# The first two units of the first batch with a 128-row third factor, filter copies without a double write, and second-factor reads ahead of the x loads

## The chip, the cores and the metric

The kernel runs on one core of a Trainium2 chip. The metric is the device time of one execution in microseconds (us), the median of several runs. The engines are named as in the profile: PE (TensorE, with PEld for its weight loads), DVE (VectorE), ACT (ScalarE), POOL (GpSimd) and SP (SyncE, which issues nearly all DMAs). SPq and POOLq are the DMA queues of SP and POOL. A DMA that waits for a semaphore holds up everything behind it on its queue.

## The reference

A spectral filter over the sequence, then a two-layer network with ELU:

```python
# x (8, 3008, 256); filt_r, filt_i (1505, 256)
X = np.fft.rfft(x, axis=1)
Y = X * (filt_r + 1j * filt_i)[None]
y = np.fft.irfft(Y, n=3008, axis=1).astype(np.float32)   # (8, 3008, 256)
# moe_w_in (256, 2048), moe_w_out (2048, 256); both arrive in 64-bit floats
h = y.reshape(24064, 256) @ moe_w_in
g = np.where(h > 0, h, np.exp(np.minimum(h, 0)) - 1)
out = (g @ moe_w_out).astype(np.float32)                 # (24064, 256)
```

## The kernel before

3008 = 47 x 64, and the two transforms are done as products with small tables. For each batch `b` there are four steps. The first factor (`x_load`, `x_unit`, `a_unit`) goes over the 64 positions and writes `z` to DRAM (`z_write`, line 309). The second factor reads `z` back by frequency (`z_read`, line 315), multiplies with its table (`b_unit`, line 384), with the filter (`re_mult` to `im_sums`, DVE), and with the back table (`bi_unit`, line 456); `y_write` (line 467) writes the rows to `yds[b]` in DRAM. The third factor reads them by `n1` (`y_read`, line 480) with a table `tn` (`tn_read`, line 473), and `n_unit` (line 495) makes the time-domain rows of six units `m` of a batch, each of 4 `n1` pairs. The network takes each unit in four parts `q` of the hidden width. Unit and part together are a *quad*, 24 for a batch.

The network's products use a seven-product scheme on 2x2 blocks. `n_sums` (lines 505 to 515) makes the block sums that the scheme needs from the unit's result; `up_steps` (line 538) does seven products with `w_in` in the order 1, 2, 6, 5, 7, 3, 4, then ELU on ACT and DVE; `down_steps` (line 620) does seven products with `w_out`. `c_unit` and `o_unit` combine and store (line 669). All matmuls are in 32-bit floats; each shows as two records in the profile.

`n_unit` as it is: the rows of frequency stand in two halves of 64 partitions, even and odd, and every product is one of four 64x64 tiles of PE, 32 matmuls in all. It yields `even` and `odd` parts in two banks, both complete only at the end; `n_sums` joins them with five DVE instructions, the first over two blocks at once. The first up product needs the result of that first instruction.

The first batch is started by its own functions (lines 245 to 371, 808 to 907): `a_first`, `t_first`, `b_first`, `bi_first`, with `y_write_first` at its end. Then come `y_read(0, 0, ...)` in two parts (line 884), the last weight blocks (`w_fetch(14)`, `w_fetch(15)`), some vector work on weights (`w_split`, `w_float`, `w_join`), warming matmuls (line 898), `x_load(1, 0)` and `(1, 1)`, `n_unit(0, 0)` and `n_sums(0, 0)`. The weights come as 64-bit floats and are turned into 32-bit floats on ACT and DVE; that work reaches into the first four quads.

Nothing is reordered by a scheduler. The order is written by hand: `at(quad, place, fn, ...)` puts a call into a plan, where place 0 is the middle of the quad, 1 its end and 2 and 3 spots between its products. The main loop goes over the quads and emits products and planned calls. All SP queue entries thus stand in program order. For batch `b`, whose quads start at `t + PER` with `t = (b - 1) * PER`, the plan makes the second factor during the quads of the batch before: `a_unit`, `z_write` and the next `x_load`s from quads `t + 0` (for batch 1: 2) to `t + 4`, `z_read` at `t + 5` place 0 for the first pair of groups, `b_unit` at `t + 6` place 1. At quad 4 the order on SP was `z_write` (4 DMAs), two `x_load`s (14 DMAs), and then, from quad 5, `z_read` (8 DMAs).

`f_pairs` (lines 768 to 776) runs at quads 1 to 4 and lays the filter out anew in DRAM, from `fd` to `fp`. For `u == 0` it wrote row 0 of the second half twice: zeros for all groups (`nil_d`), and then the true row for group 0. The second write waits for the first.

Of the kernel before, what the change touches and what calls it, by code (L numbers as in the profile page):

```python
# [26 lines left out]
P = 128  # L27
# [4 lines left out]
K2 = 32  # L32
# [9 lines left out]
def _make_tables():  # L42

    n2, k2 = np.arange(N2), np.arange(K2)
    ta, tn = np.zeros((P, H, P)), np.zeros((P, H, P))
    for i in range(H):
        for h in range(2):
            if h and i == 0:
                continue  # L60
            n1 = N1 - i if h else i
            th = 2 * np.pi * (((N1 * n2[:, None] + n1) * k2[None]) % N) / N
            c, s = np.cos(th), -np.sin(th)
            c[:, 0], s[:, 0] = 1.0, 1.0 - 2.0 * (n2 % 2)
            sign = -1.0 if h else 1.0
            r = slice(h * 64, h * 64 + 64)
            for p, v in enumerate((c, sign * s, s, sign * c)):
                ta[r, i, p * 32:p * 32 + 32] = v
                tn[p * 32:p * 32 + 32, i, r] = v.T
    tf = np.ascontiguousarray(ta.reshape(P, H, 4, K2).transpose(0, 1, 3, 2)).reshape(P, H, P)  # L70
    tb = ta.reshape(2, 2, 32, NXC, 2, 2, 4, 16, 2)[:, 0].transpose(3, 0, 1, 2, 4, 7, 5, 6)
    ta = np.ascontiguousarray(tb).reshape(P, H // 2, P)
    i = np.arange(H)[:, None]
    gb, gr, gi = (np.zeros((P, 2, 64)) for _ in range(3))
    q = np.arange(N1)[None]
    th = 2 * np.pi * ((i * np.where(q < 24, q, 70 - q)) % N1) / N1
    c, s = np.cos(th), np.sin(th)
    sign = np.where(q < 24, 1.0, -1.0)
    gb[0:24, 0, :N1], gb[24:48, 0, :N1] = c, s
    gb[64:88, 0, :N1], gb[88:112, 0, :N1] = c * sign, -s * sign  # L80
    for o in (0, 64):
        gr[o:o + N1, 0, 0:24], gr[o:o + N1, 0, 24:48] = 2 / N * c.T, 2 / N * s.T
        gi[o:o + N1, 0, 0:24], gi[o:o + N1, 0, 24:48] = 2 / N * (c * sign).T, -2 / N * (s * sign).T
    k1 = np.arange(24)[None]
    t0 = 2 * np.pi * ((i * k1) % N1) / N1
    t3 = 2 * np.pi * ((i * (32 + 64 * k1)) % N) / N
    c0, s0, c3, s3 = np.cos(t0), np.sin(t0), np.cos(t3), np.sin(t3)
    gb[0:24, 1, 0:24], gb[24:48, 1, 24:48] = c0, c3
    gb[64:88, 1, 24:48], gb[88:112, 1, 0:24] = -s3, -s0

    m0, m3 = np.full((24, 1), 2 / N), np.full((24, 1), 2 / N)
    m0[0] = m3[23] = 1 / N
    s0[:, 0] = s3[:, 23] = 0.0
    gr[0:24, 1, 0:24], gr[24:48, 1, 24:48] = m0 * c0.T, m3 * c3.T
    gi[0:24, 1, 24:48], gi[24:48, 1, 0:24] = -m0 * s0.T, -m3 * s3.T

    fb, bb = np.zeros((P, 2, 32)), np.zeros((P, 2, 4, 32))
    for p in range(4):  # L100
        r = slice(32 * p, 32 * p + 24)
        fb[r, 0, :24] = (-1.0 if p == 3 else 1.0) * gb[24 * (p % 2):24 * (p % 2) + 24, 0, 0:24]
        q = (0, 24, 64, 88)[p]
        k = 24 if p in (1, 2) else 0
        fb[r, 1, :24] = gb[q:q + 24, 1, k:k + 24]
    for o in range(0, P, 32):
        for p, (t, c) in enumerate(((gr, 0), (gr, 24), (gi, 0), (gi, 24))):
            bb[o:o + 24, 0, p, :24] = t[0:24, 0, c:c + 24]

    bb[0:24, 1, 0, :24], bb[0:24, 1, 1, :24] = gr[0:24, 1, 0:24], gr[24:48, 1, 24:48]  # L110
    bb[0:24, 1, 2, :24], bb[0:24, 1, 3, :24] = gi[24:48, 1, 0:24], gi[0:24, 1, 24:48]
    pairs = np.concatenate([fb.reshape(P, 64), bb.reshape(P, 2 * P)], 1)
    lie = np.concatenate([2 * np.arange(24), 2 * np.arange(24) + 1])
    gb[:, :, lie] = gb[:, :, :48].copy()
    for t in (gr, gi):
        for o in (0, 64):
            t[o + lie] = t[o:o + 48].copy()
    gf = np.zeros_like(gb)
    for o in (0, 64):
        gf[o:o + 48] = gb[o:o + 48].reshape(2, H, 2, 64).swapaxes(0, 1).reshape(48, 2, 64)  # L120
    tn = tn.reshape(4, K2 // 2, 2, H, 2, 2, 32)[..., 0, :] * np.array([1.0, -2.0])[:, None, None, None]
    tn = np.ascontiguousarray(tn.transpose(2, 1, 0, 3, 4, 5)).reshape(P, H, 64)
    once = np.stack([np.eye(P), gf.reshape(P, P)], 1)
    return [t.astype(np.float32) for t in (ta, tn, np.stack([gb, gr, gi], 1), tf, once, pairs)]


def order(m):
# [5 lines left out]
def kernel(  # L133
# [8 lines left out]
):  # L142
    nc = tc.nc

    ta_d, tn_d, gs_d, tf_d, once_d, pairs_d = [
        nc.inline_tensor(t, name=n + "_t").ap()
        for t, n in zip(_make_tables(), ("ta", "tn", "gs", "tf", "once", "pairs"))
    ]

    def pool(name, bufs, **kw):  # L150
# [311 lines left out]
    def y_write(b, g):  # L462
# [3 lines left out]
        for p in range(4):  # L466
            nc.sync.dma_start(yds[b][4 * g:4 * g + 8, 24 * p:24 * p + 24, :].rearrange("u r d -> r u d"),
                              t[32 * p:32 * p + 24])

    def tn_read(b, m):  # L470
        w = tnp.tile([P, 4, P], FP32, tag="tn", name="tn").rearrange("p a (q t) -> p (a q) t", t=64)[:, 0:4]
        tns[b, m] = w
        nc.sync.dma_start(w, tn_d[:, 4 * m:4 * m + 4, :])

    def y_read(b, m, *parts):
        t = t4s[b, m] = t4p.tile([P, 4, D], FP32, tag="t4", name="t4")
        for k in parts or (slice(0, K2),):
            for r in range(2):
                o = 64 * r
                nc.sync.dma_start(t[o + 2 * k.start:o + 2 * k.stop].rearrange("q i d -> q (i d)"),  # L480
                                  yds[b][k.start + r:k.stop:2].rearrange("k (p i) d -> k p (i d)", p=4)
                                  [:, :, 4 * m * D:4 * m * D + 4 * D])

    def half(m):

        return 224 if m == 0 else 256

    def n_unit(b, m):
        t, w, h = t4s.pop((b, m)), tns.pop((b, m)), half(m)
        ps = [bank("psn", (P, 2, 256)) for _ in range(2)]  # L490
        for q, i in enumerate(order(m)):
            for dh in range(2):
                for c in range(2):
                    for (_, p), r in zip(ps, HALVES):
                        nc.tensor.matmul(p[ts(c, 64), dh, ts(q, 64)], t[r, i - 4 * m, ds(dh * P + 64 * c, 64)],  # L495
                                         w[r, i - 4 * m, :], start=True, stop=True)
        even, odd, both = (yp.tile([P, 2, 256], FP32, tag=n, name=n)[:, :, 0:h] for n in ("y0", "y1", "yb"))
        t2 = yp.tile([P, 256], FP32, tag="yt", name="yt")[:, 0:h]
        ys[b, m] = {1: both[:, 0], 2: both[:, 1], 3: even[:, 1], 4: odd[:, 1], 5: odd[:, 0], 6: t2, 7: even[:, 0],
                    "even": even, "odd": odd, "both": both}  # L500
        for t, (k, p) in zip((even, odd), ps):
            nc.scalar.activation(out=t, in_=p[:, :, 0:h], func=AXT.Copy)
            banks.append(k)

    def n_sums(b, m, *parts):
        even, odd, both, t2 = (ys[b, m][k] for k in ("even", "odd", "both", 6))
        steps = ((both, odd, -0.5, even, ALU.add), (even[:, 1], odd[:, 1], 0.5, even[:, 1], ALU.add),
                 (t2, even[:, 1], 1.0, odd[:, 0], ALU.subtract), (even[:, 0], t2, 1.0, both[:, 0], ALU.subtract),
                 (odd[:, 1], both[:, 1], 1.0, t2, ALU.subtract))
        for i in parts or range(5):  # L510
            o, x, c, y, op = steps[i]
            if c == 1.0:
                nc.vector.tensor_tensor(out=o, in0=x, in1=y, op=op)
            else:
                nc.vector.scalar_tensor_tensor(out=o, in0=x, scalar=c, in1=y, op0=ALU.mult, op1=op)  # L515
# [252 lines left out]
    def f_pairs(c, u):  # L768

        src = fd.rearrange("g a q c u d -> (g a) q c u d")[:, :, c, u, :]  # L770
        dst = fp.rearrange("g (a u) k c h d -> (g a) u k c h d", u=2)[:, u, :, c, :, :]
        nc.sync.dma_start(dst[:, :, 0, :], src[:, 0:48:2, :])
        nc.sync.dma_start(dst[:, 1:24, 1, :], src[:, 1:46:2, :])
        nc.sync.dma_start(dst[:, 0, 1, :], nil_d)
        if u == 0:
            nc.sync.dma_start(dst[0, :, 1, :], src[0, 1:48:2, :])

    with tc.manual_schedule():
# [152 lines left out]
        for b in range(B):  # L931
            t = (b - 1) * PER
            if b > 0:
                for c, s in enumerate((2, 2, 3, 3, 4, 4) if b == 1 else (0, 0, 3, 3, 4, 4)):
# [4 lines left out]
                    if c % 2:  # L939
                        for k in (c - 1, c):  # L940
                            at(t + s, 1, z_write, b, k)
                        for k in (c - 1, c):
                            nb, nxt = (b, k + XBUFS) if k + XBUFS < NXC else (b + 1, k + XBUFS - NXC)
                            if nb < B:
                                at(t + s, 1, x_load, nb, nxt)
                for g in range(0, NG, 2):
                    s = t + 6 + 2 * g
                    opens.update((s + 1, s + 4))
                    for k in (g, g + 1):
                        at(s - 2, 1, f_read, b, k)  # L950
                        at(s - 1, 0, z_read, b, k)
                    at(s, 1, b_unit, b, g)
                    at(s + 1, 2, re_mult, b, g)
                    at(s + 1, 1, re_sums, b, g)
# [81 lines left out]
```

## Time and profile before

| | us |
|---|---|
| median of 3 runs | 2572.96 |
| lowest, highest | 2567.81, 2576.67 |
| profiled execution, whole | 2571.72 |
| its span (first to last instruction) | 2569.9 |
| PE busy in the span | 2525.8 |
| DVE busy | 2069.0 |
| ACT busy | 1545.1 |
| POOL busy | 159.5 |
| n_unit(0, 0): first matmul, most of them from | 86.59, 87.70 |
| first up product | 90.97 |
| first b_unit (batch 1) | 180.98 |

All times inside the profile are counted from the start of the span. The profile's page gives busy time of each engine, the chain of work that ended last (followed back from the last instruction), groups of instructions and DMA issues. The trace can be asked further: for instructions in order of time, for what an engine waited for, and for busy time in given stretches, with the clock that PE was granted (PEclk, 1.00 is full) and the share of time in which the core's 16 DMA engines were busy. The end of a matmul is modelled, so a PE that stands still shortly between matmuls can still show as busy; the start times tell it.

### The profile page before, as it was taken

The page shows a single profiled execution, that of the slowest core. Times are in us where ns is not written, and L with a number is a line of the kernel's source. Part 1 is how long each engine was busy: PE and PEld are TensorE (multiplying, and loading weights), DVE is VectorE, ACT ScalarE, POOL GpSimd, SP SyncE. Part 2 cuts the span into 40 slices and gives each one's busy share as a digit, 9 for nine tenths or more (in the row PEclk, how much of TensorE's full clock was granted, in tenths as well). Part 3 has the DMA queues.
Part 4 walks back from the last instruction along what each step waited for, and adds up shares of the span by engine and source line. Part 5 has one row for each costly group of instructions (what it writes and reads, how often), then busy time and mean ns, then how long its engine had stood idle before and what let it go on. Part 6 is the DMA issues. An engine that isn't in the chain of part 4 may idle for free.

```text
span 2569.9 us, 44172 instructions
## 1 busy us (share of the span) xinstructions
PE 2525.8 (98%) x16778; PEld 2167.7 (84%) x16778; DVE 2069.0 (81%) x3580; ACT 1545.1 (60%) x2715; POOL 159.5 (6%) x315
## 2 busy tenths in 40 slices
PE   6899999999999999999999999999999999999998
PEld 4688889888898888988889888888888888898887
DVE  6878887788877888788887888778897788876766
ACT  6665655666566655665566656566656655555554
POOL 5000100010000000000000000000000011000000
PEclk8999999999999999999999999999999999999999
DMA  9563213422234231433215231243213322110010
GB/s 279 166 177 79 69 26 91 130 68 57 49 89 118 59 74 44 111 85 75 60 40 148 67 81 36 75 122 82 57 44 83 85 63 68 36 46 19 19 28 17
DMA packets 229948, 200.36 MB, mean 78 GB/s; under 512 B 129418, under 2 KB 202314, under 8 KB 229736
## 3 DMA queue, kind: packets, MB, share of 16 engines
q1 hardware_dynamic: 214376, 166.65, 26.2%
q0 software_dynamic: 14000, 30.44, 4.2%
q8 instruction: 132, 2.16, 0.4%
q10 hardware_dynamic: 1360, 0.46, 0.1%
q14 instruction: 80, 0.66, 0.1%
HBM read 125.58 MB, written 78.17 MB: 79 GB/s over the span
## 4 chain that ended last, share of the span: by engine, by line
PE 96%; DMA 2%; DVE 1%; issue 0%; SPq 0%; ACT 0%; DVEq 0%; ACTq 0%
PE po L620 45%; PE phs L538 25%; PE phd L538 13%; PE pha L538 6%; PE psn L495 2%; PE pf L384 2%; PE psa L235 2%; PE pv L456 1%; DMA xc<-in_x_dram 1%; DMA x<-in_x_dram 0%; DMA yd<-t 0%; PE po L331 0%; PE po L297 0%; PE psr L331 0%; PE psa L278 0%
## 5 line engine op out<-in xcount | busy, mean ns | idle before, releaser
L620 PE MATMUL po<-g,wo 128*128 128x256 f32 (+1 forms) x5376 | 1319.1, 378 | 0.0
L620 PEld LDWEIGHTS po<-g,wo 128*128 128x128 f32 x5376 | 1013.2, 190 | 164.9 <-issue 50.5
L549 ACT ACTIVATE g<-phs 128x512 f32<-128x512 f32 (+1 forms) x576 | 338.7, 588 | 739.9 <-PE phs L538 737.9
L556 ACT ACTIVATE e<-e 128x512 f32<-128x512 f32 (+1 forms) x768 | 477.2, 621 | 24.3
L560 DVE SCALAR_TENSOR_TENSOR g<-e,g 128x512 f32<-128x512 f32 (+1 forms) x576 | 387.6, 673 | 13.6 <-ACT e L556 13.2
L546 DVE TENSOR_TENSOR g<-phd,g 128x512 f32<-128x512 f32 (+1 forms) x384 | 258.9, 674 | 168.0 <-ACT e L556 110.2
L538 PE MATMUL phd<-y,wi 128*128 128x256 f32 (+1 forms) x1536 | 388.6, 376 | 3.4 <-DVE g L546 3.4
L538 PE MATMUL phs<-y,wi 128*128 128x256 f32 (+1 forms) x1536 | 387.8, 375 | 0.6 <-ACT g L549 0.6
L555 ACT ACTIVATE e<-g 128x512 f32<-128x512 f32 (+1 forms) x576 | 354.5, 615 | 35.8 <-DVE g L546 27.1
L538 PEld LDWEIGHTS phd<-y,wi 128*128 128x128 f32 x1536 | 291.2, 190 | 39.3 <-DVE g L546 7.0
L538 PEld LDWEIGHTS phs<-y,wi 128*128 128x128 f32 x1536 | 292.1, 190 | 33.7 <-ACT g L549 1.2
L560 DVE SCALAR_TENSOR_TENSOR g<-e,phs 128x512 f32<-128x512 f32 (+1 forms) x192 | 130.0, 677 | 114.6 <-ACT e L556 114.6
L538 PE MATMUL phs<-yb,wi 128*128 128x256 f32 (+1 forms) x768 | 194.9, 377 | 1.8 <-DVE yb L515 1.8
L538 PE MATMUL phs<-yt,wi 128*128 128x256 f32 (+1 forms) x768 | 194.4, 376 | 0.9 <-ACT g L549 0.9
L538 PE MATMUL pha<-yb,wi 128*128 128x256 f32 (+1 forms) x768 | 194.6, 376 | 0.0
L555 ACT ACTIVATE e<-phs 128x512 f32<-128x512 f32 (+1 forms) x192 | 112.2, 584 | 111.5 <-PE phs L538 111.4
L546 DVE TENSOR_TENSOR g<-pha,g 128x512 f32<-128x512 f32 (+1 forms) x192 | 129.5, 674 | 46.6 <-PE pha L538 46.6
L538 PEld LDWEIGHTS phs<-yb,wi 128*128 128x128 f32 x768 | 144.0, 191 | 21.2 <-DVE yb L515 2.0
L538 PEld LDWEIGHTS phs<-yt,wi 128*128 128x128 f32 x768 | 146.6, 191 | 17.6 <-ACT g L549 1.2
L538 PEld LDWEIGHTS pha<-yb,wi 128*128 128x128 f32 x768 | 146.2, 191 | 17.0 <-ACT fall L393 0.2
L325 POOL DMA_DIRECT2D fall<-fp x224 | 110.1, 499 | 728.0 <-DVE r L429 697.8
L597 DVE TENSOR_TENSOR g<-g,g 128x512 f32<-128x512 f32 (+1 forms) x192 | 130.7, 681 | 6.6
(155 smaller groups left out, 2041.2 us busy)
## 6 DMA issues: line engine op xcount, KB each, us to landing
yd<-t SPq DMA_DIRECT2D x127, 192.0 KB
t<-yd SPq DMA_DIRECT2D x94, 256.0 KB
z<-t SPq DMA_DIRECT2D x84, 256.0 KB
fall<-fp POOLq DMA_DIRECT2D x224, 96.0 KB, 3.0
t<-z SPq DMA_DIRECT2D x224, 96.0 KB
out_dram<-o SPq DMA_DIRECT2D x632, 32.0 KB
xc<-in_x_dram SPq DMA_DIRECT2D x84, 128.0 KB
xc<-in_x_dram SPq DMA_DIRECT2D x161, 64.0 KB
```

The costliest lines, as they stand in the source:

```text
L235: nc.tensor.matmul(p[o:o + 64, u, :], w[r, u, o:o + 64], src[r, u, :], start=True, stop=True)
L325: nc.gpsimd.dma_start(t[32 * a:32 * a + 24].rearrange("p c u d -> p (c u d)"), fp[g, a].rearrange("q c u d -> q (c u d)"))
L384: nc.tensor.matmul(pf[p][1][32 * a:32 * a + 32, js, :], fb[r, v, :], t2[r, js, a, :], start=True, stop=True, tile_position=(32 * p, 32 * a))
L495: nc.tensor.matmul(p[ts(c, 64), dh, ts(q, 64)], t[r, i - 4 * m, ds(dh * P + 64 * c, 64)], w[r, i - 4 * m, :], start=True, stop=True)
L538: nc.tensor.matmul(ps[:, a, 0:h], w_in[q][:, COMBO[n], a, :], y[n], start=start and a == 0, stop=True, skip_group_check=True)
L546: nc.vector.tensor_tensor(out=g[o], in0=i0, in1=i1, op=ALU.add)
L549: nc.scalar.activation(out=g[o], in_=i0, func=AXT.Copy)
L555: nc.scalar.activation(out=e, in_=src, func=AXT.Relu, scale=-1.0)
L556: nc.scalar.activation(out=e, in_=e, func=AXT.Exp, scale=-1.0)
L560: nc.vector.scalar_tensor_tensor(out=g[n], in0=es[n], scalar=1.0, in1=src, op0=ALU.subtract, op1=ALU.max)
L597: nc.vector.tensor_tensor(out=b12, in0=b22, in1=b12, op=ALU.subtract)
L620: nc.tensor.matmul(po[i][:, u, 0:h], w_out[q][:, COMBO[n], a, :], g[n][:, a, :], start=q == 0 and a == 0 and n in (1, 3, 6, 4), stop=True, ...
```

## The change

It has three parts.

1. Units 0 and 1 of batch 0 take the third factor over all 128 rows. A new table `tw` holds, for the first 8 `n1` pairs, 128 columns (both output halves) for each of the 128 rows, so the two units read 256 KB of table each instead of 128 KB. `y_read` lays the rows out in one order of 128 and issues one DMA for each part instead of two. `n_whole` does 8 matmuls of 128 rows by 128 columns, 4 to a bank, copies each bank as it is complete, and yields the four blocks themselves; `n_sums` makes the remaining sums with four DVE instructions over one block each. The first up product takes the first block directly.
2. `f_pairs` writes no row twice: for `u == 0` the shifted copy and the zeros leave group 0 out.
3. `z_read` of groups 0 and 1 is planned at quad `t + 4` place 1, behind the last `z_write` and ahead of the `x_load`s, in every batch from 1 on; that of the later groups stays.

```diff
+    tw = np.ascontiguousarray(tn[:, 0:8].reshape(4, K2, 8, 2, 2, 32).transpose(1, 0, 2, 4, 3, 5)).reshape(P, 8, P)
...
+    def whole(b, m):
+
+        return b == 0 and m < 2
+
     def tn_read(b, m):
-        w = tnp.tile([P, 4, P], FP32, tag="tn", name="tn").rearrange("p a (q t) -> p (a q) t", t=64)[:, 0:4]
+        w = tnp.tile([P, 4, P], FP32, tag="tn", name="tn")
+        if not whole(b, m):
+            w = w.rearrange("p a (q t) -> p (a q) t", t=64)[:, 0:4]
         tns[b, m] = w
-        nc.sync.dma_start(w, tn_d[:, 4 * m:4 * m + 4, :])
+        nc.sync.dma_start(w, (tw_d if whole(b, m) else tn_d)[:, 4 * m:4 * m + 4, :])
 
     def y_read(b, m, *parts):
         t = t4s[b, m] = t4p.tile([P, 4, D], FP32, tag="t4", name="t4")
         for k in parts or (slice(0, K2),):
+            if whole(b, m):
+                r = slice(4 * k.start, 4 * k.stop)
+                nc.sync.dma_start(t[r], yds[b].rearrange("k (p i) d -> (k p) i d", p=4)[r, 4 * m:4 * m + 4, :])
+                continue
             for r in range(2):
...
+    def n_whole(b, m):
+        t, w, h = t4s.pop((b, m)), tns.pop((b, m)).rearrange("p i (k t) -> p i k t", k=2), half(m)
+        rows = []
+        for dh in range(2):
+            y = yp.tile([P, 2, 256], FP32, tag="y%d" % dh, name="y%d" % dh)[:, :, 0:h]
+            k, ps = bank("psn", (P, 2, 256))
+            for q, i in enumerate(order(m)):
+                nc.tensor.matmul(ps[:, :, ts(q, 64)], t[:, i - 4 * m, ds(dh * P, P)], w[:, i - 4 * m], start=True, stop=True)
+            nc.scalar.activation(out=y, in_=ps[:, :, 0:h], func=AXT.Copy)
+            banks.append(k)
+            rows += [y[:, 0], y[:, 1]]
+        b11, b12, b21, b22 = rows
+        t = yp.tile([P, 2, 256], FP32, tag="yb", name="yb")[:, :, 0:h]
+        t2 = yp.tile([P, 256], FP32, tag="yt", name="yt")[:, 0:h]
+        ys[b, m] = {1: b11, 2: b21, 3: b22, 4: t[:, 1], 5: t[:, 0], 6: t2, 7: b12}
+
     def n_unit(b, m):
+        if whole(b, m):
+            return n_whole(b, m)
...
     def n_sums(b, m, *parts):
+        if whole(b, m):
+            b11, b21, b22, t4, t1, t2, b12 = (ys[b, m][k] for k in range(1, 8))
+            for o, x, y in ((t1, b12, b11), (b12, b22, b12), (t2, b22, t1), (t4, b21, t2)):
+                nc.vector.tensor_tensor(out=o, in0=x, in1=y, op=ALU.subtract)
+            return
...
         nc.sync.dma_start(dst[:, :, 0, :], src[:, 0:48:2, :])
-        nc.sync.dma_start(dst[:, 1:24, 1, :], src[:, 1:46:2, :])
-        nc.sync.dma_start(dst[:, 0, 1, :], nil_d)
+        g = 1 - u
+        nc.sync.dma_start(dst[g:, 1:24, 1, :], src[g:, 1:46:2, :])
+        nc.sync.dma_start(dst[g:, 0, 1, :], nil_d[g:])
         if u == 0:
             nc.sync.dma_start(dst[0, :, 1, :], src[0, 1:48:2, :])
...
                         for k in (c - 1, c):
                             at(t + s, 1, z_write, b, k)
+                        if c == NXC - 1:
+                            for k in range(2):
+                                at(t + s, 1, z_read, b, k)
                         for k in (c - 1, c):
                             nb, nxt = (b, k + XBUFS) if k + XBUFS < NXC else (b + 1, k + XBUFS - NXC)
...
                         at(s - 2, 1, f_read, b, k)
-                        at(s - 1, 0, z_read, b, k)
+                        if g:
+                            at(s - 1, 0, z_read, b, k)
```

More of the change, by code (lines that the diff above doesn't have):

```diff
@@ L123, in _make_tables @@
     once = np.stack([np.eye(P), gf.reshape(P, P)], 1)
-    return [t.astype(np.float32) for t in (ta, tn, np.stack([gb, gr, gi], 1), tf, once, pairs)]
+    return [t.astype(np.float32) for t in (ta, tn, np.stack([gb, gr, gi], 1), tf, once, pairs, tw)]
 def order(m):
@@ L143 @@
     nc = tc.nc
-    ta_d, tn_d, gs_d, tf_d, once_d, pairs_d = [
+    ta_d, tn_d, gs_d, tf_d, once_d, pairs_d, tw_d = [
         nc.inline_tensor(t, name=n + "_t").ap()
-        for t, n in zip(_make_tables(), ("ta", "tn", "gs", "tf", "once", "pairs"))
+        for t, n in zip(_make_tables(), ("ta", "tn", "gs", "tf", "once", "pairs", "tw"))
     ]
```

## The prediction

> **What bounds the kernel now.** I read the page's head and its chain first, then the waits of TensorE (PE), then the start of the main loop and the first use of each thing that the diff touches.
>
> ```profile
> PE 2525.8 (98%) x16778; PEld 2167.7 (84%) x16778; DVE 2069.0 (81%) x3580; ACT 1545.1 (60%) x2715; POOL 159.5 (6%) x315
> PE 96%; DMA 2%; DVE 1%; issue 0%; SPq 0%; ACT 0%; DVEq 0%; ACTq 0%
> ```
>
> PE sets the time: it is busy for 98% of the span and makes 96% of the chain. The list of its waits is short (15.2 us for one table at the start, then nothing above 3.4 us), and cut into stretches PE is busy for all of 160 to 2400 us. So work that other engines save counts for nothing after about 145 us, unless PE stands still behind a busy mark. The change can gain only at places where PE waits, and I looked for those.
>
> The first is the start of the loop. The chain in order of time, from the last write of y to the third product:
>
> ```profile
> 81.35 0.97 SPq L480
> 84.05 2.70 DMA t<-yd
> 86.75 3.54 issue
> 90.97 1.86 PE phs L538 x4
> 92.83 1.49 PE pha L538 x4
> 94.33 1.26 PE phs L538 x4
> ```
>
> The reader sees SP issuing the second-factor reads (L480), the last one landing, then 3.54 us of the unit `n_unit(0, 0)` with its copies and its first sum, then three up products of 4 matmul records. Later products of that shape take 0.76 us; these take 1.26 to 1.86, and busy time by stretch, cut where the granted clock (PEclk) changes, shows why:
>
> ```profile
> 81.54:84.95 3.41, 1.81 (x5) 0.50 (x3) 3.34 (x8) 3.38 (x6) 0.00 (x0) 1.00 0.37 102
> 84.95:88.37 3.42, 0.97 (x47) 0.89 (x51) 1.76 (x4) 2.10 (x4) 0.00 (x0) 1.00 0.94 275
> 88.37:91.78 3.41, 1.59 (x35) 1.37 (x25) 1.41 (x3) 0.98 (x2) 0.00 (x0) 0.50 0.93 269
> 91.78:95.19 3.41, 3.41 (x10) 3.09 (x10) 1.45 (x4) 0.54 (x1) 0.00 (x0) 0.50 0.67 176
> 109.75:144.00 34.25, 30.83 (x260) 27.59 (x259) 33.28 (x62) 24.07 (x43) 0.52 (x1) 1.00 0.39 113
> 183.94:187.35 3.41, 3.41 (x30) 1.51 (x5) 0.78 (x2) 1.80 (x6) 0.00 (x0) 0.50 0.20 37
> ```
>
> Columns: length, then busy time of PE, weight load, DVE, ACT, POOL, then PEclk, DMA share, GB/s. After a stretch with 0.97 us of PE work the clock is 0.50 for two stretches of 3.41 us. From 109.75 to 144 DVE is busy for 33.28 of 34.25 us: there DVE paces, and PE waits for it (2.82 us at 121.2, 0.60 at 137.7).
>
> The second place is the first `b_unit` (L384), against the same unit one batch later:
>
> ```profile
> 181.05 4.51 PE pf L384 x28
> 185.55 1.97 PE po L620 x4
> ...
> 494.48 1.65 PE pf L384 x20
> 496.13 1.06 PE po L620 x4
> ```
>
> 4.51 + 1.97 = 6.48 us against 2.71. The weight loads of that unit wait four times for `DMA t<-z`, and the next stretch runs at clock 0.50 (last row above). SyncE's (SP's) timeline tells why the reads are late:
>
> ```profile
> 162.88 3.49 SPq L309 DMA_DIRECT2D z<-t  x4
> 177.10 3.83 SPq L315 DMA_DIRECT2D t<-z  x8
> SPq L776 <- DMA fp<-nil_t: 7.2, 2, 3.6
> ```
>
> Between the writes of z and the reads stand 14 DMAs of two x loads. The third row, from the waits of SP, is the copy that writes a row twice.
>
> **The change, part by part.**
>
> (1) Reads of `y` for unit (0, 0): two DMAs instead of four. Four issues run from 81.35 to 84.67 (3.32 us). Two of them cost 1.0 + 0.65, so the last starts about 1.7 us sooner, but the first now carries both halves (448 KB). The four reads' packets flowed from 83.0 to 86.3; at the 277 GB/s of the first 68 us, 480 KB take 1.7 us. I take 1.6 us: unit start 87.70 to 86.1. Bounds: 0.7 (only one short issue saved) and 2.4 (all but the first issue saved). The table of the unit is 256 KB instead of 128: 128 KB more at 277 GB/s are 0.5 us of DMA, at 39 us. It lies ahead of filter reads that land by 60 and are used until 72 at DVE's pace; uncovered it costs 0.5.
>
> (2) The unit itself. Now 64 records of 64x64 take 1.09 us at full clock (162.49), and both banks end together. After: 8 matmuls, 16 records, of 128 rows by 128 columns. Nearest row: transposes of 128x128, 31 in 3.57 us, 0.115 each, so 1.84 us, the first bank after 0.92. The first product needs only the first bank's copy (0.54 us), which ends at 1.56, before PE is free at 1.84. From unit start to first product: 1.9 us instead of 3.27, a gain of 1.4 (bounds 0 with all of it at half clock, 1.6). The second product needs the second copy, at 2.5, while the first runs until 2.7; the third needs three of the four subtractions, 0.39 us each, ending near 3.3, before 3.4. So the sums lie under the products. If they came late, 0.4 us each.
>
> The Trainium skill speaks against this part: "TensorEngine Tiling (Array Packing)", Overview, says that a 64-row, 64-column problem runs on four independent tiles at once. By that rule the new form, twice the columns through the whole array, would cost twice 1.09, a loss of 1.1 us per unit; by the transposes' row it is 0.75.
>
> (3) The clock. PE idles from 83.35 (end of the warming matmuls) to 86.1: 2.75 us instead of 3.24 + 0.81 + 1.82 with little between. In this trace stretches of 3.41 us with 0.67, 1.15 and 0.97 us of PE work were followed by a drop, those with 1.69, 1.81, 1.92 not; 2.59 did not lift it again, 2.83 did. With the cut between, 1.4 us of work, an idle time of 2.75 trips a stretch in (2 x (2.75 - 2.0) + 0.66) / 3.41 = 6 of 10 positions of their borders. No drop: the three products take 3 x 0.76 = 2.3 instead of 4.6, a gain of 2.3. One drop: 3.41 us at half clock, which gives 1.7 of it back. The likelier is one drop: gain 0.6 (bounds -1.1, two drops, and 2.3).
>
> On this the Trainium skill, "TensorE: Matmul & The Clock Gate", Part 1, says the gate halves the clock after a whole idle window of some 3.4 us, free-running. By that an idle 2.75 never trips it and the sum below is 1.7 us better; the rows above, dropped with work in the window, decide.
>
> (4) The same for unit (0, 1), at 111.5 us. PE +0.75 (1.84 for 1.09), in the stretch where PE waits 3.4 us for DVE: hidden; otherwise 0.75. DVE: five sums from 114.30 to 116.61, 2.31 us, become four of 256 elements at 0.39 = 1.57. DVE paces here, so 0.75 us gain. Everything DVE waits for in 92 to 110 (15.2 busy of 23.25 us) comes from PE and ACT, so the start's gain is carried through; weight blocks 14 and 15, queued behind the reads, come 1.6 earlier too.
>
> (5) Filter copies (L776): the last copy of each pair no longer waits for the two before, 3.57 and 3.54 us of SP. Behind the first, SP is idle until 128.7 anyway. Behind the second stand the reads of unit (0, 2), the z writes and two x loads, then the z writes at 162.88, all 3.5 us sooner. No engine waited for them: 0 by itself. It is cover for (6).
>
> (6) z reads ahead of the x loads, in all seven batches. Eight reads are issued, 3.83 us, after waiting for z to land: packets of the four writes drained by 169.0, so some 4 us after 166.4. Even unshifted they are issued at 170.5 to 174.3 and land about 2.7 later, at 177; with (5) and the shift of PE's own writes, near 169. PE comes to `b_unit` at about 175. Gain 6.48 - 2.71 = 3.8 us (bounds 1.5, if they still land 2 us late, and 3.8). Behind the waiting read stand the x loads of the next batch (used some 20 quads later), the output stores and the read of unit (0, 3). That was issued by 194.76 for 204.79; with 2.7 of landing it had 7.3 us to spare. It moves by +4 (the wait) - 3.5 (5) and by PE's own shift, PE by about -8: some 3 to 4 us stay. In later batches reads issued at 481.4 were used at 494.4, without a stall: nothing to gain, and SP waits 4.5 us for the output tile, which takes the new wait up.
>
> **Sum.** -1.6 - 1.4 - 0.6 - 0.75 - 3.8 = -8.1 us on the profiled execution (2571.72 us, of which 2569.9 span): 2563.6. It ran 1.2 us below the median shown, 2572.96, which the forecast undercuts by 0.36%. A difference under 0.3%, 7.7 us, is about what a measurement of this kernel can't tell from none.
>
> **Rivals.**
> The clock stays up, the rest as said: -9.8, 2561.9. Chance 0.22; the forecast itself 0.38.
> The start's gain is lost on DVE: if the vector work of 92 to 110 were bound by something fixed (a weight block, a copy on ACT), only (4) and (6) remain: -4.6, 2567.2. For it: DVE is near full right behind. Against: it idles 8 of 23 us there, behind PE and ACT. 0.18.
> The z reads do not cure the stall, because z lands late among the filter reads of POOL that flow at 168 to 176 us, or the clock still drops there: -4.3 - 1.5 = -5.8, 2565.9, or with no cure -4.3, 2567.4. 0.16.
> Slower: SP, held by the z wait, delivers a later unit's read too late in every batch. In batch 2 the read of the unit at 514.4 is issued by 502.6: with 2.7 landing, 9.1 us to spare, and 4.5 in front of the output stores. It decides from a wait of 13.6 us; with 16.5 us in each of the six later batches it costs 6 x 2.9 = 17, less 8: 2581. Against it: four z writes drain within 3 us of their last issue. 0.06.
>
> **Range and chances.** Best bounds together: -2.4 - 1.6 - 2.3 - 0.75 - 3.8 = -10.9, 2560.9; runs shown lie up to 3.9 below the profiled one, so 2557. Above, the rivals at 2567 with the same scatter: 2571. Chances: faster 0.58 (forecast and kept clock, less scatter), same 0.36, slower 0.06.
>
> **What would show it.** The unit's first matmul near 86 and two issues of reads before it; the first product within 2 us of it; one or no stretch at clock 0.50 behind it; PE's 2.82 us wait for DVE at 121 cut by half or more; no wait on `fp<-nil_t`; z reads issued before the x loads, and `pf` at 1.65 with clock 1.00 behind it. Wrong if `pf` still takes over 3 us, if products still start 3 us behind the unit, or if a new PE wait appears at unit (0, 3).

## The result, and the profile after

The changed kernel takes 2562.81 us (median of 9 runs, 2559.58 to 2564.17), the kernel before 2570.93 us (9 runs, 2567.81 to 2576.67). The ratio is 0.9966, with a 95% interval of 0.9956 to 0.9977: faster by 0.34%, or 8.1 us on the medians. The forecast was 2563.6 within 2557 to 2571, faster. The profiled spans fall from 2569.9 to 2560.5 us, by 9.4.

Busy time of the engines, from the page of the kernel after, shows nothing of it but 5.3 us less of PE:

```profile
PE 2520.5 (98%) x16682; PEld 2161.5 (84%) x16682; DVE 2067.5 (81%) x3578; ACT 1545.2 (60%) x2715; POOL 159.5 (6%) x315
```

The chain of the kernel after, in order of time (start, length, step), answers to the two chains shown of before:

```profile
80.97 4.21 DMA t<-yd
...
85.46 1.14 PE psn L506 x8
...
87.05 0.53 ACT y L507
...
87.63 1.02 PE phs L572 x4
88.65 0.76 PE pha L572 x4
89.41 0.92 PE phs L572 x4
...
175.14 1.65 PE pf L385 x20
176.79 1.06 PE po L654 x4
```

Between the unit and the first product stand one half of the unit's matmuls and one copy; no vector sum is left in that path, as the change intended. Products take 0.76 to 1.02 us instead of 1.26 to 1.86. The first `b_unit` takes 1.65 + 1.06 = 2.71 us instead of 6.48. Busy time by stretch (length, PE, weight load, DVE, ACT, POOL, PEclk, DMA share, GB/s) shows that the granted clock stayed at 1.00 through the start, and in the stretch where DVE paces (last row):

```profile
80.85:84.26 3.41, 2.05 (x5) 0.57 (x3) 3.31 (x9) 3.35 (x7) 0.00 (x0) 1.00 0.62 175
84.26:87.67 3.41, 2.06 (x17) 1.90 (x17) 2.08 (x6) 3.38 (x7) 0.00 (x0) 1.00 0.96 298
87.67:91.08 3.41, 2.78 (x13) 2.20 (x14) 2.98 (x8) 1.48 (x3) 0.00 (x0) 1.00 1.07 266
104.50:138.00 33.50, 31.22 (x212) 28.32 (x211) 32.58 (x61) 24.06 (x43) 0.52 (x1) 1.00 0.41 122
```

SyncE's timeline (start, length, instruction, count) shows two read issues of y where there were four, and the reads of z at 159.45, ahead of the x loads, where they were issued at 177.10:

```profile
80.97 1.18 SPq L487 DMA_DIRECT2D t<-yd  x2
...
152.61 3.72 SPq L310 DMA_DIRECT2D z<-t  x4
159.45 3.22 SPq L316 DMA_DIRECT2D t<-z  x8
```

The list of PE's waits (total, times, longest) has the one wait for reads of y ahead of the unit, and the wait for DVE at unit (0, 1), 2.82 us before, at 1.7:

```profile
PE psn L506 <- DMA t<-yd: 2.6, 1, 2.6
PE phd L572 <- DVE g L580: 2.3, 2, 1.7
```

Put together by the same marks in both traces: the first read of y is issued 0.38 us earlier (81.35, 80.97; between 79.26 and 84.35 over all fourteen profiles of this case, so this is scatter); from there to the unit's third matmul record it takes 4.79 us for 6.35; from there to the first product 1.87 for 3.27; from there to the fourth product 3.31 for 5.24; from the fourth product to `b_unit` 0.64 less; `b_unit` itself 3.8 less. That makes 9.7 us, of which 0.2 is lost again behind the last matmul. From the first product behind this `b_unit` to the last matmul both kernels take 2374.0 us, and so does every kernel below, within 0.3 us. So all that this case decides lies in the first 188 us.

### The profile page after: what moved, and what is told of

The parts are those of the page before. It is cut to its first block, busy times and chain, and to the rows that moved or that the text cites. A ratio compares the mean times of both kernels' runs of the same rounds, so it can differ in the third digit from the quotient of the medians.

```text
span 2560.5 us, 43982 instructions
## 1 busy us (share of the span) xinstructions
PE 2520.5 (98%) x16682; PEld 2161.5 (84%) x16682; DVE 2067.5 (81%) x3578; ACT 1545.2 (60%) x2715; POOL 159.5 (6%) x315
## 4 chain that ended last, share of the span: by engine, by line
PE 97%; DMA 2%; DVE 1%; issue 0%; ACT 0%; SPq 0%; DVEq 0%; ACTq 0%
PE po L654 45%; PE phs L572 25%; PE phd L572 13%; PE pha L572 6%; PE psn L524 2%; PE psa L236 2%; PE pf L385 1%; PE pv L457 1%; DMA xc<-in_x_dram 1%; PE po L332 1%; DMA x<-in_x_dram 0%; PE po L298 0%; PE psr L332 0%; DMA t<-yd 0%; PE psa L279 0%
## 5 line engine op out<-in xcount | busy, mean ns | idle before, releaser
L572 PE MATMUL phd<-y,wi 128*128 128x256 f32 (+1 forms) x1504 | 380.3, 375 | 0.0
L572 PEld LDWEIGHTS phd<-y,wi 128*128 128x128 f32 x1504 | 284.8, 190 | 35.1 <-DVE g L580 2.7
L572 PE MATMUL pha<-yb,wi 128*128 128x256 f32 (+1 forms) x736 | 186.0, 375 | 0.0
L572 PEld LDWEIGHTS pha<-yb,wi 128*128 128x128 f32 x736 | 139.3, 190 | 16.7 <-ACT fall L394 0.5
```

The source lines that it names most:

```text
L572: nc.tensor.matmul(ps[:, a, 0:h], w_in[q][:, COMBO[n], a, :], y[n], start=start and a == 0, stop=True, skip_group_check=True)
```

## Which part brings the time

The three parts were run alone (`only_whole` is part 1, `only_f` part 2, `only_z` part 3), and two of the pairs (`no_f` is parts 1 and 3, `no_z` parts 1 and 2). A part is taken out by putting back the lines of before:

```diff
     def whole(b, m):
-        return b == 0 and m < 2
+        return False
```
```diff
-        g = 1 - u
-        nc.sync.dma_start(dst[g:, 1:24, 1, :], src[g:, 1:46:2, :])
-        nc.sync.dma_start(dst[g:, 0, 1, :], nil_d[g:])
+        nc.sync.dma_start(dst[:, 1:24, 1, :], src[:, 1:46:2, :])
+        nc.sync.dma_start(dst[:, 0, 1, :], nil_d)
```
```diff
-                        if c == NXC - 1:
-                            for k in range(2):
-                                at(t + s, 1, z_read, b, k)
...
-                        if g:
-                            at(s - 1, 0, z_read, b, k)
+                        at(s - 1, 0, z_read, b, k)
```

What was expected of `only_whole`:

> The kernel before with part 1 alone (two units over 128 rows). Theory (the parts add): the start gives about 6 us of the 8 (in the changed kernel's trace the first b_unit comes 5.9 us earlier, at 175.1 for 181.0), and the 4.5 us stall in that b_unit stays, since PE's and SP's work move together: ratio near 0.998, b_unit at 175 to 176, pf piece above 4 us with clock 0.50 behind it. Rival (the start's gain is lost on DVE or was start-up scatter): first b_unit at 179 or later, ratio 0.9995 or more. Rival (the earlier start alone cures the stall): pf at 1.65, ratio below 0.9972.

of `only_z`:

> The kernel before with part 3 alone (z reads ahead of the x loads). Theory: start as before (first product at 90 to 91.5), reads issued some 4 us behind the last z write, near 170 to 174, landed by 177, so pf is 1.65 and the clock behind it 1.00: 3.8 us less, ratio near 0.9985. Rival (part 2 is what brings the reads forward): with the 3.5 us wait on the double write left in, the reads land after 181 and pf stays above 3 us: ratio 0.9995 or more.

of `only_f`:

> The kernel before with part 2 alone (no row written twice). Theory of the prediction: no engine waits for these copies, 0 by itself, ratio 1.000 within its interval. Rival: the 3.5 us that SP gains stand ahead of the z reads too, which are issued at 173.6 instead of 177.1 and land by 180.2 instead of 183.7, before or just as PE comes at 181.0: then pf falls to 1.65 to 2.5 and this part alone gives 3 to 3.8 us, ratio 0.9985 to 0.9988.

of `no_f`:

> The changed kernel with the double write put back (parts 1 and 3 alone). Theory: z reads about 3.5 us later than in the changed kernel (159.5 to 163), landed near 169, b_unit at 175: no stall, same time as the changed kernel (ratio to before 0.9966). Rival (part 2 is needed as cover): a stall in pf or a new wait of PE at the unit read behind the output stores (third-factor unit 3, then at 195), 1 us or more, ratio 0.997 or above.

and of `no_z`, written when the four had been measured:

> The changed kernel without part 3: z reads behind the x loads again. Theory of the prediction (the moved reads cure the stall, worth 3.8 us): pf over 3 us, ratio near 0.998. Rival, after the three runs with one part each (any 3 us of lead cures it, and parts 1 and 2 each give that): z reads end 5 us or more before b_unit, pf 1.65, ratio as the changed kernel, 0.996 to 0.9966.

Measured (first product and first weight load of `b_unit` in us from the start of the span; "lead" is the time from the end of the last issue of a z read to that weight load):

| kernel | median us | ratio (95% interval) | first product | `b_unit` | lead | `pf` piece |
|---|---|---|---|---|---|---|
| before | 2571.12 | 1 | 90.97 | 180.97 | 0.04 | 4.51 |
| part 1 alone | 2563.09 | 0.9963 (0.9951 to 0.9976) | 88.42 | 175.85 | 3.61 | 1.65 |
| part 2 alone | 2569.19 | 0.9990 (0.9981 to 0.9999) | 92.61 | 182.79 | 3.47 | 1.65 |
| part 3 alone | 2568.79 | 0.9986 (0.9977 to 0.9995) | 92.55 | 182.49 | 7.49 | 1.65 |
| parts 1 and 3 | 2561.26 | 0.9959 (0.9946 to 0.9972) | 86.64 | 174.07 | 9.57 | 1.65 |
| parts 1 and 2 | 2563.02 | 0.9963 (0.9951 to 0.9976) | 87.32 | 174.76 | 5.53 | 1.65 |
| all three | 2562.81 | 0.9966 (0.9956 to 0.9977) | 87.63 | 175.07 | 12.40 | 1.65 |

The 2571.12 is the kernel before beside the first four; in that of `no_z` it took 2572.72, and the ratio of each row is to the runs beside it. Part 1 alone brings all of the gain. The other two bring about 0.1% each by themselves and nothing that can be measured beside part 1. So the parts do not add up: 0.37 + 0.10 + 0.14 is 0.61%, against 0.34% together.

The reason can be read in the `pf` column: each part alone removes the whole stall at `b_unit`. SyncE's timelines of part 1 alone and of part 2 alone:

```profile
155.17 3.58 SPq L310 DMA_DIRECT2D z<-t  x4
168.78 3.46 SPq L316 DMA_DIRECT2D t<-z  x8
```
```profile
175.51 3.81 SPq L316 DMA_DIRECT2D t<-z  x8
```

and the weight loads of `pf` in the latter (start, length, instruction, and in brackets the idle time before the first):

```profile
182.79 0.81 PEld L385 LDWEIGHTS pf<-t,pairs 24*32 24x32 f32 x40 [0.33 <-issue]
```

In part 2 alone the eight reads are issued until 179.3 and the 40 weight loads then run through at 182.79 without waiting for a DMA. A lead of 3.5 us is enough; the kernel before had 0.04, and `before_warm` below, with 0.65, still takes 3.22 us for the `pf` piece. Part 2 gives it by less waiting in SP's queue: in its profile PE comes to `b_unit` 1.8 us later than before, yet the reads are issued 1.6 us sooner, 3.4 us between them, near the 3.6 of the one wait on `fp<-nil_t` that lies behind 128 us. Part 1 gives it because SP's queue follows PE there: it waits for ACT's copy of the first factor's output until its z write (128.74 before, 123.61 with part 1 alone), and then works through the same DMAs up to the z reads, 48.4 us long before and 45.2 with part 1 alone. The first 5.1 us of its shift of 8.3 are PE's own; the 3.2 us by which the queue itself ran shorter are spread over the three groups of x loads (0.9, 1.5 and 0.6 us) and the wait for the double write (0.2), so no single wait accounts for them.

The table also tells why parts 2 and 3 alone gain 2 us and not the 3.8 of the stall. With the old unit PE reached `b_unit` at 180.97 in the profile of before, but at 182.5 to 182.9 in the three other profiles with that unit (parts 2 and 3 alone, and `before_warm` below). PE comes early there or late, and in before the unit can't end sooner than its data: its first product behind `b_unit` starts at 187.35, against 185.11 with part 3 alone and 185.41 with part 2 alone. The differences, 2.2 and 1.9, are those of the spans within 0.1 (2567.6 and 2568.0 against 2569.9).

## The clock at the start

The changes of the clock in one trace lie whole multiples of 3.413 us apart (in before at 43.99, 88.37 and 95.20: 13 and 2 of them). So its stretches have fixed borders, and only a stretch cut at these borders tells what the clock followed. The stretches shown at the start of the loop are cut so; in the kernel after, the last change ahead of the start is at 43.30, which puts the borders at 80.85, 84.26 and 87.67.

With the old unit four profiles of four show the clock at 0.50 near the unit: from 86.4 and 86.9 with parts 3 and 2 alone, where the unit has hardly begun, and from 88.4 and 89.9 in before and `before_warm`, behind it. Two theories: the idle time of PE ahead of the unit does it, or the unit itself. In `before_warm` the idle time is filled, by three more warming matmuls in the kernel before:

```diff
-            for k in range(7):
+            for k in range(10):
```

> The kernel before with ten warming matmuls instead of seven, which then end near 86 and leave PE no idle stretch before the unit. Theory (2.3 us of the start's gain is the granted clock): no stretch at 0.50 behind 85, the three first products 2.3 us instead of 4.6, first b_unit 2 to 2.5 us earlier behind the unit's start; if the stall there is gone with it, ratio near 0.9975, if it stays near 0.999. Rival (the clock is not the price, the shorter path is): the products are faster but the later ones wait for ACT and DVE as before, b_unit no earlier than 1 us, ratio 0.9995 or more.

It took 2571.35 us, a ratio of 1.0 (0.9991 to 1.0009). Busy time by stretch:

```profile
83.09:86.50 3.41, 3.41 (x10) 1.33 (x8) 3.34 (x8) 3.38 (x7) 0.00 (x0) 1.00 0.74 206
86.50:89.91 3.41, 1.29 (x64) 1.05 (x62) 0.69 (x2) 1.71 (x4) 0.00 (x0) 1.00 1.03 293
89.91:100.15 10.24, 8.57 (x22) 7.23 (x23) 5.18 (x13) 2.94 (x6) 0.00 (x0) 0.50 0.77 200
```

PE was busy for all of the stretch ahead of the unit, and the clock fell all the same, for three stretches, behind the stretch with the unit's 64 small matmuls and the wait for its sums. So the long idle time ahead of the unit was not needed for the drop; the unit, 1.33 us of waiting before it and the wait for its sums are enough. More warming is no remedy for the old form.

With the new unit the same knob was turned both ways, to 3 warming matmuls (`after_cold`) and to 9 (`after_warm`):

```diff
-            for k in range(7):
+            for k in range(3):
```

> The changed kernel with three warming matmuls instead of seven, so PE idles some 6 us ahead of the unit. Theory (the granted clock is a part of the start's gain, worth 1.7 to 2.5 us): a stretch at 0.50 ends behind the unit's start, the unit takes 3.7 us instead of 2.0 or the first products 1.3 to 1.9 instead of 0.8 to 1.0 each, and b_unit comes 89 to 90 us behind the first product or the unit starts it late: 1.7 to 3 us slower than the changed kernel, ratio to before 0.9973 to 0.9977. Rival (the clock costs nothing, ACT and DVE pace the first products anyway): ratio 0.9965.

> The changed kernel with nine warming matmuls instead of seven, which end 1.8 us later, near 84.6. Theory: in most runs of the changed kernel the clock stays up anyway (4 of 5 profiles of kernels with its start), so 0 to 0.5 us faster in the median and a smaller spread, ratio near 0.996. Rival (the warming matmuls end too late and delay the unit): unit starts 0.5 us or more later behind the first read's issue.

`after_cold` took 2564.41 us (ratio 0.9979, 0.9966 to 0.9992), `after_warm` 2564.13 (0.9970, 0.9958 to 0.9981). PE's timeline of `after_cold` has the unit after 6.47 us of idle time, and by stretch the clock is at half for 6.83 us:

```profile
87.27 3.75 PE L506 MATMUL psn<-tn,t 128*128 128x128 f32 x16 [6.47 <-DMA t<-yd]
```
```profile
81.37:84.78 3.41, 0.00 (x0) 0.00 (x0) 3.31 (x7) 3.38 (x7) 0.00 (x0) 1.00 0.45 107
84.78:91.61 6.83, 4.34 (x19) 4.30 (x20) 3.17 (x8) 4.46 (x8) 0.00 (x0) 0.50 1.02 305
```

At half clock the unit takes 3.75 us, at full clock (`after_warm`) 2.02. From the first read's issue to the first product it takes 7.8 us, against 6.3 and 6.7 in `after_warm` and after, but 7.0 to 8.1 in four others whose clock stayed up (parts 1 alone, 1 and 2, 1 and 3, and `pool_sums` below). So what the drop costs the first product is not shown by these. The medians, 2564.41 and 2564.13, can't be told apart. `after_warm` gains nothing over the 7 of the change.

## The reads of y

The prediction put the gain of part 1's reads down to two issues instead of four. Two kernels put four back: `four_reads` cuts each part in two by rows, `column_reads` by columns (112 or 16 rows of 2 KB each).

```diff
-                nc.sync.dma_start(t[r], yds[b]...[r, 4 * m:4 * m + 4, :])
+                n = (r.start + r.stop) // 2
+                for r in (slice(r.start, n), slice(n, r.stop)):
+                    nc.sync.dma_start(t[r], yds[b]...[r, 4 * m:4 * m + 4, :])
```
```diff
-                nc.sync.dma_start(t[r], yds[b]...[r, 4 * m:4 * m + 4, :])
+                for i in range(0, 4, 2):
+                    nc.sync.dma_start(t[r, i:i + 2], yds[b]...[r, 4 * m + i:4 * m + i + 2, :])
```

> The changed kernel with each part of the y reads cut in two DMAs again (four issues as in the kernel before, rows in the new order; the compute is that of the changed kernel). Theory (term 1): the unit starts 1.3 to 2 us later behind the first read's issue (81.0 to 85.5 in the changed kernel), PE's idle stretch grows from 2.6 to 4 us or more, and the clock falls to 0.50 behind it, so the first product's chain loses another 1.7: 1.5 to 3.5 us slower than the changed kernel. Rival (the transfer, not the issues, sets the landing): the unit starts within 0.4 us of the changed kernel's.

> The changed kernel with each part of the y reads cut in two by columns: four issues, each waiting for the same writes as the single one (the halves by rows in the run before let the first start early). Theory (term 1, the issues set the landing): from the first read's issue to the unit 6 to 6.6 us instead of 4.8 (changed kernel: 80.97 to 85.75), 1.3 to 2 us slower than the changed kernel when the clock stays up. Rival (the transfer sets it): below 5.2 us, same time as the changed kernel. [...]

`four_reads` took 2562.67 us (ratio 0.9963, 0.9950 to 0.9975), `column_reads` 2562.24 (0.9967, 0.9955 to 0.9980). As a test of the number of issues `four_reads` is flawed: its first read covers rows that are written early, so it was issued at 79.26, before the last write of y had landed, and the second only at 81.16. Its 6.80 us from first issue to unit can't be set beside the others. `column_reads` waits for the same writes as the change. SyncE's timeline of it:

```profile
80.41 1.73 SPq L488 DMA_DIRECT2D t<-yd  x4
```

Four issues take 1.73 us, 0.32 to 0.42 each, and from the first of them to the unit it is 4.49 us, no more than the 4.79 of the change with two (0.32 and 0.30 for the issues). Before, the four took 0.97, 0.85, 0.65 and 0.63. So the number of issues is not what counted: each issue of the old row order, 56 or 8 rows in two dimensions, cost about twice as much or more, and its packets started over 3.7 us (83.05 to 86.79) against 2.2 (81.92 to 84.14). Which of the two ends the unit's wait was not separated. What the reads gain comes with the rows laid out as one order of 128.

How much of it reaches the first product is set by ACT. ACT's timeline of the kernel after:

```profile
85.68 1.47 ACT L749 ACTIVATE rq<-rq,edges 128x512 f32<-128x512 uint32 x2
87.05 1.01 ACT L507 ACTIVATE y<-psn 128x448 f32<-128x448 f32 x2
```

The unit's first half ends at 86.59, but ACT, whose instructions stand in the written order, is busy with the weights (L749) without a pause from 78.32 on and starts the copy 0.46 us later; in before the copy starts 0.07 us behind the unit. With part 1 alone, parts 1 and 2, parts 1 and 3, and in `four_reads` and `pool_sums`, the copy starts 0.93 to 1.21 us behind its half, and PE waits 0.61 to 0.90 us for it. Only in `after_warm` and in the three profiles whose clock fell does it start right behind the half. So a median here can't show what a few tenths of a microsecond in the reads are worth.

`column_reads` is also one of two kernels with the new unit at 7 warming matmuls whose clock fell:

```profile
81.17:84.58 3.41, 1.23 (x4) 0.34 (x3) 3.38 (x8) 3.38 (x7) 0.00 (x0) 1.00 0.83 237
84.58:88.00 3.42, 3.42 (x17) 3.42 (x18) 1.44 (x4) 2.12 (x4) 0.00 (x0) 0.50 1.03 316
```

A stretch with 1.23 us of PE work was followed by a drop here; in the kernel after the two stretches at the start have 2.05 and 2.06 us, and none followed.

## Unit (0, 1), and the engine that paces there

`one_unit` gives unit (0, 1) its old form back; `pool_sums` moves four sums of weight columns (1.67 us on DVE, at 113.16) to POOL, to see whether PE's remaining wait for DVE goes with them.

```diff
     def whole(b, m):
-        return b == 0 and m < 2
+        return b == 0 and m < 1
```
```diff
-                                    (2, 2, w_sums, 13), (2, 1, w_join, 14), (2, 1, w_join, 15),
+                                    (2, 2, w_sums, 13, nc.gpsimd), (2, 1, w_join, 14), (2, 1, w_join, 15),
```

> The changed kernel with unit (0, 1) in the old form (unit (0, 0) in the new one). Theory: PE saves 0.75 us in that unit and DVE has 0.75 us more; DVE paces there, so PE's wait of 1.7 us near 116 grows to about 3 and the first b_unit comes 0.6 to 0.8 us later behind the first product: 0.7 us slower than the changed kernel. Rival (PE paces, the new unit costs more than it gives): b_unit 0.7 us earlier.

> The changed kernel with one set of weight sums (w_sums(13), four instructions, 1.67 us of DVE) on POOL, where such a set takes 3.0 us. Theory (DVE paces from 104 to 138 and PE's waits of 1.7 and 0.6 us there are its price): PE's waits near 116 and 131 together shrink by 1.2 to 1.7 us, first b_unit 86 us behind the first product instead of 87.4, ratio 0.9955 to 0.996. Rival (the waits come from ACT, or POOL's sums are late for the products with those weights): waits as before or a new one of PE on POOL, no gain or a loss of 1 us or more.

`one_unit` took 2564.29 us (ratio 0.9970, 0.9961 to 0.9979). PE's timeline has the wait back at its old size:

```profile
88.53 3.75 PE L506 MATMUL psn<-tn,t 128*128 128x128 f32 x16 [2.99 <-DMA t<-yd]
...
124.12 1.02 PE L572 MATMUL phd<-yb,wi 128*128 128x224 f32 x4 [2.82 <-DVE g L580]
```

So the new form of this unit is what shortened it, 2.82 to 1.7. Its first unit ran at half clock and started late (first read at 84.35), so its span of 2567.2 says little about the second unit. From its fourth product to `b_unit` it takes 1.40 us more than the kernel after (85.53, 84.13), but the clock fell once more there, behind this wait (0.50 from 125.20 to 128.61). The median's 1.3 to 1.5 us over its neighbours is inside the intervals.

`pool_sums` took 2564.01 us (0.9972, 0.9961 to 0.9984), and the wait stayed at 1.75 us. DVE's timeline beside POOL's four sums:

```profile
113.61 1.00 DVE L222 TENSOR_TENSOR sd<-xc 128x512 f32<-128x512 f32 x1
114.64 1.10 DVE L223 TENSOR_TENSOR xc<-xc 128x512 f32<-128x512 f32 x1
115.67 1.21 DVE L222 TENSOR_TENSOR sd<-xc 128x512 f32<-128x512 f32 x1
116.92 1.10 DVE L223 TENSOR_TENSOR xc<-xc 128x512 f32<-128x512 f32 x1
```

and the same part of DVE's timeline in the kernel after:

```profile
113.16 1.67 DVE L781 TENSOR_TENSOR wi<-wi 128x256 f32<-128x256 f32 x4
114.75 0.68 DVE L222 TENSOR_TENSOR sd<-xc 128x512 f32<-128x512 f32 x1
115.47 0.69 DVE L223 TENSOR_TENSOR xc<-xc 128x512 f32<-128x512 f32 x1
```

The four x sums take 4.41 us instead of 2.74: DVE got slower by exactly the 1.67 us that it was relieved of.

## Why the prediction was right, step by step

The total was right, and the two places where time was to be gained were the right ones. The steps below it were not all right.

(1) Reads, 1.6 us: measured 1.56 in this pair of profiles. The size was right and the step behind it wrong. "Two of them cost 1.0 + 0.65" counted issues at their old price; the two new ones cost 0.32 and 0.30, and `column_reads` has four issues and the same time. It is the shape of a read that counted. The pair flatters the size: in the three other profiles with the old unit it is 7.3 to 7.6 us from the first issue to the unit's third record, with the new one 4.5 to 5.6 (`four_reads` left out), so about 2.5 us is more usual. Two numbers of the step were off: the reads move 512 KB (128 packets of 4 KB), not 480, and their packets flowed until 86.9, not 86.3.

(2) The unit, 1.9 us to the first product, a gain of 1.4: measured 1.87 and 1.40 from the third record, the mark that suits the kernel before; from the unit's first record it is 2.17. The 16 records take 2.0 us, against 1.84 from the row of the transposes. That the copy "ends at 1.56, before PE is free" did not hold: it ended 2.12 us behind the first record, because the step did not ask what stood ahead of it on ACT. Unit (0, 1) takes 1.95 instead of 1.16, a loss of 0.8, as by the row's 0.75. The estimate of 1.1 after the Trainium skill's "TensorEngine Tiling (Array Packing)", Overview, was too high.

(3) The clock, one drop, a gain of 0.6: wrong in this profile, where no stretch dropped and the gain was 1.93. That is the first rival, whose sum of -9.8 is what the spans show (-9.4). Of the nine profiles with the new unit and 7 or 9 warming matmuls two dropped, where the step said 6 positions of 10. Its rule, a cut at 1.4 us of work in a stretch, held: between 75 and 200 us of all fourteen profiles the clock fell behind stretches with 0.00, 0.82, 0.97, 1.08, 1.08, 1.23, 1.29 and 1.30 us and behind none with 1.57 or more, save one, ahead of 183.94 in before, where PE stood waiting for z behind marks that count as busy. What was off is the idle time put into the rule: 2.75 us, where five of the profiles have 1.51 to 1.90, and the kernel after has 2.56, which the border at 84.26 happened to divide. By the Trainium skill's "TensorE: Matmul & The Clock Gate", Part 1, a wholly idle window halves the clock; that covers the 0.00 (`after_cold`) and not the seven other drops.

(4) Unit (0, 1): DVE's saving of 0.75 appears as 0.64, with PE's own 0.8 hidden, as said; the wait was cut by 1.1 us and not by half. `one_unit` shows it come back.

(5) The copies, 0 by themselves: wrong, they are worth 0.10% (0.01 to 0.19) alone, because the 3.6 us of SP's queue are enough to cure the stall of (6). Only beside the other parts are they worth nothing.

(6) The z reads, 3.8 us: right in this profile, but for the wrong part. The step priced the stall with SP's old times and PE's, and gave the cure to the moved reads; it did not ask whether (1) or (5), which it had just moved, had cured it already. `no_z` has no stall and the same time. And the 3.8 itself belongs to one execution in which PE came early to `b_unit`; `before_warm`, with PE later, loses 1.6 in `pf`, and alone the cure brings about 2.

The errors in the reads and the clock and that in the size of the stall lie on opposite sides, so the median's 8.1 meets the forecast's 8.1 more closely than its terms deserve. The rival of a slower kernel had SP held by the wait for z: SP waits 3.1 us for it (to 159.45; the step had 4), and no new PE wait appears, at unit (0, 3) or in later batches. DVE's side did not swallow the gain of the start: 5.3 us at the fourth product are 5.9 at `b_unit`.

No version beats the changed kernel beyond its interval. The best median, parts 1 and 3 without 2 (2561.26), is 1.5 us below and inside it.

## What to carry to other kernels

When several edits pull at one stall, price the stall once and ask for each edit what is left of it when the others are in; a stall of 3.8 us that 3.5 us of lead cures is cured by any of them. A stall read from one profile has the size of that execution: where the engine's arrival scatters by 1 to 2 us, so does the stall. In a start-up path look at the shape of each DMA before its count, and at how many instructions stand between data and the first consumer: the whole-array form does more work on PE, and yet its first product starts 1.1 to 1.4 us sooner behind the unit's start. Ask too what the engine that copies the result has still to do: here ACT's weight work became the last thing that the first product waited for. And cut the busy time at the clock's own borders before a rule is read from it; shifted by 1 us, a stretch of the kernel after shows 1.10 us of work where the clock saw 2.05.

## What the runs showed of the hardware

Reads of 56 and of 8 rows in two dimensions took 0.97 to 0.85 and 0.65 to 0.63 us to issue, reads of 112 and of 16 rows in one dimension 0.30 to 0.42.

Elementwise work with two inputs on POOL slows DVE's: sums of 128x512 took 1.00 to 1.21 us for 0.68 to 0.69 while POOL ran, and POOL's own 0.73 to 1.18. The Trainium skill's "GPSIMD Engine Reference", section "1. Specifications", names the shared SBUF interfaces and contention with DVE instructions of two SBUF inputs; here a move of 1.67 us off DVE gave back nothing.

The granted clock changed only at borders 3.413 us apart. In all fourteen traces, from end to end, a stretch between borders at full clock was followed by half clock if PE's marks fill at most 1.56 us of it, and by full clock if they fill 1.57 or more, with the one exception named above; a stretch at half clock was followed by half clock up to 2.78 us and by full clock from 2.81 on. Idle time alone does not tell it: the clock fell with 2.18 us ahead of the unit, all in one stretch (`column_reads`), and stayed with 2.56 divided by a border.
